# A new order of the first 520 steps in a fused attention and feed-forward kernel: two early holds and twelve more left out, two parts of w_in moved behind the third values

## The chip, the cores and the metric

The kernel runs on one core of a Trainium2 chip. The metric is the device time of one execution in microseconds (us), given as the median of several runs. The engines are TensorE (PE; PEld is its weight load), VectorE (DVE), ScalarE (ACT), GpSimd (POOL) and SyncE (SP). SP, POOL and, for three early transfers, ACT issue the DMAs; 16 DMA engines carry them.

## The reference

Inputs are q, k and v of 8 batches, 12 heads, 448 positions and 64 dimensions, w_in (768 x 2048) and w_out (2048 x 768), all float32; tau is 0.1.

```python
q_n = q / (norm(q, axis=-1) + 1e-6)
k_n = k / (norm(k, axis=-1) + 1e-6)
scores = q_n @ k_n.T / tau                # per batch and head, 448 x 448
attn = softmax(scores)
x = (attn @ v), heads side by side        # 3584 tokens x 768
h = x @ w_in
out = maximum(0.01 * h, h) @ w_out        # 3584 x 768
```

## The kernel before

Work goes by pairs of heads, 48 in all (s = 0 to 47, six in a batch), and by quads j of four heads. The first twelve pairs (two batches) use one layout, the later ones are loaded two pairs at a time as units. The feed-forward part goes by chunks c of tokens, two to a pair of batches: even chunks have 384 columns, odd ones 512.

Nothing is scheduled automatically. The string ORDER lists about 1,260 steps; the loop at the end of the kernel calls them one by one, and each engine runs its instructions in exactly that sequence. Semaphores only make an instruction wait for its data or for a buffer. So the order is the whole plan, and a waiting instruction holds up all that stands behind it on its engine. The steps, by name in ORDER:

- lq.s loads pair s of q and k on SP (from pair 12 on, the q or the k of two pairs), for s < 12 in four transfers (L238 to L241), later in two (L230). It uses a pool of four buffers, so a load waits until the normalise of an older pair has read its buffer. The pairs 0 to 5 are loaded ahead of ORDER (L211, L219, L220).
- lv.j and lr load the values and their last 64 rows, wi.i (L182) a quarter of w_in and wo.half (L188) half of w_out, or half of a half with a range; all on POOL. wi.0 and wi.1 hold the even and the odd row blocks (kt) of the columns m = 0 to 7, wi.2 and wi.3 those of m = 8 to 15. lg loads values for the later batches.
- sq.s.p squares on POOL (L306, later L300; p = 0 is q, 1 is k), sa on ACT; su sums on DVE (L319, L316). qf and uf do this for pair 0 in three pieces (L324, L330): main q (qf.0.0.3), main k (qf.1.0.3) and the last 64 rows of both (qf.0.3.4). ro.s takes the roots on ACT (L336, L337), no.s normalises on DVE into qn (L342 to L359).
- tp.s transposes on TensorE (L374), tc.s copies the result with DVE and ta with ACT (L390). k.s.i makes scores (L427), x.s.i the exps on ACT (L438). to.j and pr.j.e are the sums and products with the values on TensorE (L450), ln and in the inverse of the sums on ACT (L462, L466), sc.j.e scales into xT on DVE (L478).
- f.c.m and any kt behind it is the product with w_in (L588), r.c.m the leaky ReLU on ACT (L602), s.c.t.lo.hi the product with w_out (L624), o its copy out on DVE and the store on SP (L640, L648).
- q, y, g, gl, gi, gx, tt and td do the same as k, x, to, pr, ln, in, sc and the transposes for the units of the later batches.
- w.n are n matmuls on a constant tile (L695) whose result isn't used; tg lets TensorE's output banks be given out without a split in halves.
- hp.s is a hold: a copy of one element of the normalised pair s on POOL (L704), which makes what stands behind it on POOL wait for no.s. hs.s is the same for SP's queue, a transfer of one element (L701). hr reads an element of pair 0's remainder on POOL (L707).

```python
    def hold_loads(s):
        nc.sync.dma_start(out=behind, in_=qn[s][0:1, 6, 0, 0:1])

    def hold(s):
        gp.tensor_copy(out=seen, in_=qn[s][:, 6, 0, 0:1])
```

Of the kernel before, what the change touches and what calls it, by code (L numbers as in the profile page):

```python
# [764 lines left out]
```

## Time and profile before

| | |
|---|---|
| median of 3 runs | 414.89 us (414.45 to 415.11) |
| the profiled execution | 414.45 us |
| its span, first to last instruction | 412.7 us |
| TensorE busy | 403.0 us (98%) |
| granted TensorE clock | 1.00 throughout |
| ACT, DVE, POOL busy | 245.8, 262.2, 117.9 us |
| w_out's first half: issue, time to landing | 32.45, 22.97 us |
| first product with w_out (L624) | 55.47 us |

The span counts from the first instruction to the last; the execution's own time is 1.75 us longer. Busy time is the time in which an engine has at least one instruction in flight. In lists of instructions the columns are start, length, engine, line, operation and tiles, and behind "x" how many of them were merged; in brackets stands the idle time before and what ended it. In the list of waits the columns are the total, the number and the longest. In the chain that ended last each piece has a start and a length.

### The profile page before, as it was taken

The page shows a single profiled execution, that of the slowest core. Times are in us where ns is not written, and L with a number is a line of the kernel's source. Part 1 is how long each engine was busy: PE and PEld are TensorE (multiplying, and loading weights), DVE is VectorE, ACT ScalarE, POOL GpSimd, SP SyncE. Part 2 cuts the span into 40 slices and gives each one's busy share as a digit, 9 for nine tenths or more (in the row PEclk, how much of TensorE's full clock was granted, in tenths as well). Part 3 has the DMA queues.
Part 4 walks back from the last instruction along what each step waited for, and adds up shares of the span by engine and source line. Part 5 has one row for each costly group of instructions (what it writes and reads, how often), then busy time and mean ns, then how long its engine had stood idle before and what let it go on. Part 6 is the DMA issues. An engine that isn't in the chain of part 4 may idle for free.

```text
span 412.7 us, 11078 instructions
## 1 busy us (share of the span) xinstructions
PE 403.0 (98%) x4662; PEld 211.5 (51%) x4679; DVE 262.2 (64%) x424; ACT 245.8 (60%) x431; POOL 117.9 (29%) x125
## 2 busy tenths in 40 slices
PE   7899999999999999999999999999999999999997
PEld 2335555544555555544455555554455555554565
DVE  6987769757758556765484877699978591310021
ACT  4897886367937785667865679515854735104400
POOL 2978474164416032532240623330010000000000
PEclk9999999999999999999999999999999999999999
DMA  7999999767387852683555756382052210010032
GB/s 186 247 215 195 227 227 167 213 171 157 92 184 212 206 132 50 168 241 93 104 136 155 178 158 161 83 203 83 2 99 76 80 41 0 2 75 2 2 114 76
DMA packets 41976, 53.81 MB, mean 130 GB/s; under 512 B 12486, under 2 KB 32326, under 8 KB 41926
## 3 DMA queue, kind: packets, MB, share of 16 engines
q1 hardware_dynamic: 25734, 41.01, 35.7%
q0 software_dynamic: 15504, 11.80, 20.0%
q8 instruction: 36, 0.59, 0.6%
q10 hardware_dynamic: 688, 0.30, 0.2%
q14 instruction: 14, 0.11, 0.1%
HBM read 45.61 MB, written 11.01 MB: 137 GB/s over the span
## 4 chain that ended last, share of the span: by engine, by line
PE 83%; DMA 10%; DVE 3%; SPq 2%; issue 1%; POOL 1%; DVEq 0%
PE ps L624 33%; PE ps L588 32%; PE ps L538 8%; PE ps L492 7%; DMA w_out_sb<-in_moe_w_out_dram 6%; DMA qk_h<-in_q_dram 2%; PE ps L450 2%; DMA qk_h<-in_k_dram 1%; DMA xT<-in_q_dram 1%; DVE shared L508 1%; PE ps L524 1%; PE ps L427 1%; SPq L211 0%; SPq L219 0%; DVE qn L359 0%
## 5 line engine op out<-in xcount | busy, mean ns | idle before, releaser
L624 PE MATMUL ps<-w_out_sb,hT 128*128 128x384 bf16 (+1 forms) x912 | 151.7, 324 | 0.3 <-DMA w_out_sb<-in_moe_w_out_dram 0.3
L588 PE MATMUL ps<-xT,w_in_sb 128*128 128x384 bf16 (+1 forms) x753 | 149.4, 352 | 1.1 <-issue 0.5
L500 ACT ACTIVATE pe<-ps 128x896 bf16<-128x896 f32 x126 | 109.9, 917 | 54.4 <-PE ps L492 54.2
L624 PEld LDWEIGHTS <-hT 128*128 128x128 bf16 x912 | 86.4, 98 | 64.3 <-issue 10.1
L588 PEld LDWEIGHTS <-w_in_sb 128*128 128x128 bf16 x768 | 73.2, 98 | 73.4 <-issue 7.8
L602 ACT ACTIVATE hT<-ps 128x384 bf16<-128x384 f32 (+1 forms) x128 | 64.4, 549 | 62.1 <-PE ps L588 44.1
L300 POOL TENSOR_TENSOR sq<-qk_h 128x896 f32<-128x896 f32 x36 | 64.8, 1805 | 77.6 <-DMA qk_h<-in_q_dram 39.5
L640 DVE COPY osb<-ps 128x384 f32<-128x384 f32 (+1 forms) x57 | 30.7, 544 | 78.3 <-PE ps L624 74.7
L349 DVE TENSOR_TENSOR qn<-qk_h,r 128x896 bf16<-128x896 f32 x36 | 43.9, 1220 | 1.5
L316 DVE TENSOR_REDUCE ss<-sq 128x14 f32<-128x910 f32 x36 | 38.3, 1070 | 8.0 <-POOL sq L300 8.0
L438 ACT ACTIVATE pe<-ps 128x896 bf16<-128x896 f32 x42 | 36.3, 914 | 5.2 <-PE ps L427 5.1
L492 PE MATMUL ps<-qkT 64*32 64x448 bf16 x1008 | 36.0, 352 | 0.2 <-DVE osb L640 0.2
L508 DVE TENSOR_TENSOR shared<-shared,pe 128x896 f32<-128x896 f32 x30 | 35.5, 1215 | 0.3
L564 DVE TENSOR_TENSOR xT<-ps,rb 128x448 bf16<-128x448 f32 x32 | 18.3, 616 | 20.1 <-ACT rb L550 12.4
L400 DVE STREAM_TRANSPOSE tt<-qn 128x448 f32<-128x448 f32 x36 | 28.6, 812 | 0.5
L538 PE MATMUL ps<-pe,vq 64*32 64x448 bf16 x1008 | 27.0, 349 | 0.0
L704 POOL CAST seen<-qn 128x1 f32<-128x1 bf16 x21 | 6.6, 315 | 68.9 <-DVE qn L349 66.1
L492 PEld LDWEIGHTS <-qkT 64*32 64x32 bf16 x1008 | 12.6, 91 | 19.1 <-issue 14.7
L342 DVE TENSOR_REDUCE r<-norms 128x14 f32<-128x28 f32 x48 | 8.3, 174 | 21.7 <-ACT norms L337 21.1
L282 POOL DMA_DIRECT2D vq<-in_v_dram x20 | 12.6, 637 | 25.6 <-PE ps L492 25.6
L538 PEld LDWEIGHTS <-vq 64*32 64x32 bf16 x1008 | 14.6, 93 | 8.7 <-issue 0.6
L336 ACT ACTIVATE ss<-ss 128x14 f32<-128x14 f32 x48 | 10.3, 215 | 9.4 <-DVE ss L316 6.3
(55 smaller groups left out, 234.6 us busy)
## 6 DMA issues: line engine op xcount, KB each, us to landing
qk_h<-in_k_dram SPq DMA_DIRECT2D x36, 224.0 KB, 4.5
qk_h<-in_q_dram SPq DMA_DIRECT2D x36, 224.0 KB, 4.3
out_dram<-osb SPq DMA_DIRECT2D x20, 384.0 KB, 2.4
qkT<-tt SPq DMA_DIRECT2D x72, 56.0 KB, 2.0
qkT<-tt SPq DMA_DIRECT2D x36, 112.0 KB, 2.4
vq<-in_v_dram POOLq DMA_DIRECT2D x16, 224.0 KB, 5.0
w_in_sb<-in_moe_w_in_dram POOLq DMA_DIRECT2D x4, 768.0 KB, 9.6
out_dram<-osb SPq DMA_DIRECT2D x15, 192.0 KB, 3.4
```

Of the source, the lines that this page charges most:

```text
L300: gp.tensor_tensor(sq[:, :, :D], x, x, op=ALU.mult)
L316: nc.vector.tensor_reduce(o, sqs[s], axis=AX.X, op=ALU.add)
L349: nc.vector.tensor_tensor(qn[s].rearrange("p m d e -> p m e d"), raw[s].rearrange(f"p ({t[1:-1]} d) -> p m e d", e=n, d=D), r.rearrange(f" ...
L438: nc.scalar.activation(out=dst, in_=sc[:, :, :S], func=AF.Exp, scale=inv_tau)
L492: nc.tensor.matmul(out=sc[32 * strip : 32 * strip + 32, a, :S], lhsT=x[rows, c0 : c0 + 32], rhs=x[rows, 0:S], start=True, stop=True,)
L500: nc.scalar.activation(out=pq[u, i], in_=sc[:, :, :S], func=AF.Exp, scale=inv_tau)
L508: eng.tensor_tensor(whole[u], pq[u, 0] if i == 1 else whole[u], pq[u, i], op=ALU.add)
L538: nc.tensor.matmul(out=po[32 * strip : 32 * strip + 32, w, :S], lhsT=weights, rhs=pq[us[x if two else 0], i][rows, a, :], start=(i == 0), ...
L588: nc.tensor.matmul(out=pm[:, :n], lhsT=w_in_sb[:, kt, m * 128 : (m + 1) * 128], rhs=xT[c // 2][:, kt, c0 : c0 + n], start=(done + i == 0), ...
L602: nc.scalar.activation(out=hT[c][:, m, :n], in_=pm[:, :n], func=AF.Prelu, alpha=0.01)
L624: nc.tensor.matmul(out=po2[:, : hi - lo], lhsT=hT[c][:, m, ts * 128 : (ts + 1) * 128], rhs=w_out_sb[:, m, lo:hi], start=(m == 0), stop=(m ...
L640: nc.vector.tensor_copy(out=o[:, lo:hi], in_=bank(("s", c, ts, lo))[:, : hi - lo])
```

## The change

Only ORDER changes. Its first 534 steps become 520, from the start to the third batch's second unit (y.4.0 and all behind it are as before). Fourteen holds are left out: hp.1, 4, 8, 10, 11, 12, 13, 15, 17, 20, 22 and 23, hs.3 and hs.11. No other step is added or removed. The others are permuted, on every engine:

- The squares and sums of pair 0 begin with the last 64 rows (qf.0.3.4). ta.0.0.4 comes before ro.1.
- On POOL, lv.2, wi.3, sq.7.1, sq.6.0, wi.2 now follow sq.5.0 (before: hp.4, sq.6.0, lv.2, hr, hp.5, sq.6.1, sq.7.0, sq.7.1, wi.2, wi.3). lr.1.0.4 comes before sq.8.0 and wo.0 (before: behind wo.0 and lv.3). wo.1.0.8 comes before lv.3, and lv.4 behind wo.1.8.
- On SP, lq.9 follows lq.8 directly; lq.13 comes before lq.11; hs.9 stands behind lq.12 (before: ahead of lq.13 and lq.12).
- On DVE, no.4 comes before su.5.1; su.6 to su.8 all come before no.6; no.8 follows no.7 (before: no.9 was ahead of no.8).
- On ACT, ro.6 follows all exps of pair 5 (before: it was ahead of x.5.3), and ro.11 and ro.13 come before x.9.1 and r.0.15.
- On TensorE, the same steps stand ahead of the first product with w_out in both orders, but k.8.0 before and k.8.2 after; that first product is s.0.0.0.384 before and s.0.2.0.384 after.

The first lines of both orders (the diff's lines, cut behind the first products with w_out):

```diff
-qf.0.0.3 qf.1.0.3 uf.0.0.3 lq.6 qf.0.3.4 w.20 uf.1.0.3 uf.0.3.4 ro.0 sa.1.1 sq.2.1 sa.1.0 no.0 tp.0.4.7 su.1.0
-sq.2.0 su.1.1 tg tp.0.0.4 w.2 lr.0.0.2 ro.1 tc.0.4.7 su.2.1 lv.0 sq.3.1 no.1 su.2.0 w.2 ta.0.0.4 sq.3.0 lq.7
-k.0.1 lr.0.2.4 x.0.1 k.0.0 w.2 w.2 tp.1 k.0.2 x.0.0 w.2 tc.1 k.1.3 ro.2 no.2 su.3.0 su.3.1 x.0.2 k.1.2 x.1.3
-lv.1 k.1.1 x.1.2 x.1.1 ro.3 w.2 sq.4.1 k.1.0 tp.2 w.3 tc.2 k.2.1 k.2.2 k.2.0 x.1.0 su.4.1 to.0 x.2.2 pr.0.0
-no.3 hp.1 sq.4.0 su.4.0 x.2.1 x.2.0 ro.4 tp.3 w.2 wi.0 tc.3 ln.0 wi.1 sq.5.1 k.3.3 lq.8 su.5.1 k.3.2 k.3.1
-sq.5.0 w.2 no.4 su.5.0 hp.4 sq.6.0 x.3.3 lv.2 hr x.3.1 x.3.2 pr.0.1 tp.4 tc.4 k.3.0 ro.5 x.3.0 no.5 in.0 k.4.0
-k.4.1 hp.5 x.4.1 sc.0.0 sc.0.1 to.1 tp.5 k.4.2 ln.1 pr.1.1 pr.1.0 sq.6.1 sq.7.0 sq.7.1 tc.5 x.4.0 in.1 x.4.2
-sc.1.1 k.5.0 sc.1.0 k.5.2 hs.3 x.5.0 k.5.3 wi.2 x.5.2 f.0.1.0.2 f.0.0.0.2 k.5.1 x.5.1 wi.3 su.6.0 su.6.1
-su.7.1 f.0.1.1 f.0.1.3 f.0.0.1 ro.6 x.5.3 sq.8.0 wo.0 lv.3 f.0.2.0.1.2.3 f.0.3.0.1.2.3 to.2 pr.2.1 pr.2.0 lq.9
-ln.2 in.2 no.6 su.7.0 tp.6 sq.8.1 lq.10 sc.2.1 sc.2.0 f.0.6 sq.9.1 f.0.3.4.5 f.0.2.4.5 f.0.0.4.5 r.0.6
-f.0.1.4.5 ro.7 lr.1.0.4 r.0.2 sq.9.0 tc.6 su.8.0 su.8.1 no.7 k.6.2 k.6.0 r.0.3 f.0.4 f.0.5 x.6.2 sq.10.0 tp.7
-lq.11 sq.10.1 tc.7 r.0.1 su.9.0 su.9.1 f.0.0.3 f.0.7 r.0.4 x.6.0 r.0.5 r.0.0 ro.8 f.0.15 k.6.1 k.7.0 ro.9
-r.0.15 x.7.0 r.0.7 k.7.1 f.0.10 x.6.1 x.7.1 f.0.9 no.9 tp.9 r.0.9 r.0.10 tc.9 su.10.0 f.0.8 k.7.2 k.9.2 k.7.3
-su.10.1 x.9.2 lv.4 sq.11.1 f.0.12 f.0.11 r.0.8 ro.10 x.7.3 x.7.2 no.8 hs.9 no.10 hp.8 sq.11.0 f.0.13 f.0.14
-tp.8 r.0.13 r.0.11 lq.13 r.0.12 wo.1.0.8 r.0.14 k.9.1 tc.8 x.9.1 su.11.1 sq.13 k.9.0 to.3 su.11.0 ln.3 lq.12
-k.9.3 ro.11 k.8.0 x.9.3 x.9.0 x.8.0 tp.10 s.0.0.0.384 no.11 tc.10 k.8.1 k.10.1 k.8.2 sq.12 x.8.1 in.3 pr.3.1
-o.0.0.0.384 wo.1.8 hs.11 su.13 pr.3.0 ro.13 x.8.2 x.10.1 tp.11 s.0.1.0.384 hp.11 tc.11 k.11.0 sc.3.0 lv.5
-sc.3.1 su.12 k.11.1 k.11.2 x.11.0 x.11.1 s.0.2.0.384 lq.14 k.11.3 no.13 o.0.1.0.384 ro.12 x.11.2 k.10.2 k.10.0
-x.11.3 pr.4.1 hp.10 no.12 pr.4.0 x.10.0 to.4 x.10.2 hp.13 lq.15 sq.14 to.5 s.0.0.384.768 s.0.2.384.768 pr.5.1
-ln.5 su.14 tt.13 tt.12 ro.14 ln.4 in.4 in.5 pr.5.0 sq.15 su.15 o.0.2.0.384 no.14 td.0 lq.16 sc.4.0
-o.0.2.384.768 sc.4.1 sc.5.1 o.0.0.384.768 q.0.0 q.0.2 q.0.1 lq.18 ro.15 s.0.1.384.768 hp.12 sq.16 y.0.0 y.0.1
-y.0.2 tt.14 sc.5.0 no.15 f.1.12 f.1.15 f.1.11 f.1.1 lq.19 lq.17 r.1.12 tt.15 r.1.11 su.16 o.0.1.384.768 r.1.15
-sq.18 sq.17 sq.19 q.0.4 q.0.3 q.0.5 su.18 su.17 td.1 y.0.3 hp.15 lg.0 f.1.7 r.1.1 ro.16 no.16 y.0.4 r.1.7
...
+qf.0.3.4 uf.0.3.4 qf.1.0.3 uf.1.0.3 qf.0.0.3 uf.0.0.3 ro.0 no.0 sa.1.1 sa.1.0 sq.2.1 su.1.0 w.2 w.20 tp.0.4.7
+tc.0.4.7 su.1.1 su.2.1 sq.2.0 lr.0.0.2 tp.0.0.4 ta.0.0.4 w.2 w.2 lv.0 ro.1 w.2 sq.3.1 sq.3.0 lr.0.2.4 no.1
+sq.4.1 w.2 k.0.1 k.0.0 x.0.1 lq.6 x.0.0 w.3 su.2.0 tp.1 tc.1 lq.7 lv.1 ro.2 k.0.2 tg x.0.2 sq.4.0 k.1.1 k.1.2
+k.1.3 no.2 w.2 wi.0 su.3.1 x.1.2 x.1.3 x.1.1 w.2 su.3.0 tp.2 tc.2 w.2 su.4.1 ro.3 k.1.0 k.2.2 k.2.0 x.1.0 wi.1
+sq.5.1 sq.5.0 k.2.1 to.0 lv.2 x.2.2 x.2.0 no.3 su.4.0 wi.3 tp.3 x.2.1 pr.0.1 sq.7.1 sq.6.0 tc.3 k.3.2 wi.2
+ro.4 ln.0 x.3.2 k.3.1 k.3.0 pr.0.0 no.4 su.5.1 lq.8 su.5.0 hr x.3.0 lq.9 x.3.1 ro.5 tp.4 k.3.3 x.3.3 sq.6.1
+tc.4 k.4.0 in.0 x.4.0 no.5 sq.8.1 sq.7.0 lr.1.0.4 to.1 ln.1 sc.0.0 k.4.1 pr.1.0 k.4.2 in.1 sc.0.1 x.4.1 tp.5
+tc.5 pr.1.1 sc.1.0 k.5.3 f.0.1.0.2 sc.1.1 su.8.1 x.4.2 su.6.1 su.6.0 x.5.3 k.5.0 f.0.0.0.2 k.5.1 k.5.2 x.5.0
+x.5.1 f.0.0.1 f.0.1.3 f.0.1.1 f.0.3.0.1.2.3 f.0.2.0.1.2.3 su.7.0 su.7.1 x.5.2 sq.8.0 su.8.0 ro.6 to.2 pr.2.1
+pr.2.0 f.0.0.3 wo.0 no.6 tp.6 ro.8 ln.2 in.2 ro.7 sc.2.0 sc.2.1 f.0.7 r.0.7 f.0.0.4.5 f.0.3.4.5 f.0.2.4.5
+f.0.1.4.5 sq.9.0 sq.9.1 hp.5 tc.6 r.0.0 no.7 lq.10 r.0.1 k.6.1 k.6.0 no.8 f.0.6 sq.10.1 x.6.0 r.0.2 lq.13
+f.0.5 r.0.3 tp.7 su.9.1 wo.1.0.8 r.0.6 su.9.0 sq.10.0 r.0.5 x.6.1 lv.3 ro.9 f.0.4 tc.7 no.9 k.7.3 k.7.0 k.7.1
+r.0.4 x.7.3 tp.8 f.0.8 x.7.0 x.7.1 r.0.8 f.0.9 k.7.2 k.6.2 tp.9 tc.8 tc.9 su.10.1 f.0.11 su.10.0 lq.11 lq.12
+f.0.12 hs.9 f.0.10 x.7.2 x.6.2 sq.13 k.9.2 k.9.3 r.0.11 r.0.9 r.0.12 k.9.0 ro.10 no.10 wo.1.8 sq.11.1 to.3
+r.0.10 x.9.3 f.0.13 ln.3 sq.11.0 su.11.1 su.13 sq.12 x.9.2 f.0.14 lq.14 r.0.13 x.9.0 r.0.14 tp.10 k.8.2 k.9.1
+su.11.0 f.0.15 ro.11 no.11 ro.13 x.9.1 r.0.15 tc.10 s.0.2.0.384 x.8.2 tp.11 no.13 su.12 tc.11 o.0.2.0.384
+s.0.1.0.384 ro.12 k.11.2 k.11.1 lq.15 o.0.1.0.384 tt.13 no.12 x.11.1 x.11.2 k.8.1 s.0.0.0.384 k.8.0 sq.14 lv.4
+lv.5 x.8.1 in.3 k.10.1 x.8.0 k.10.0 pr.3.0 o.0.0.0.384 tt.12 sq.15 td.0 su.14 sc.3.0 lq.16 to.4 lq.18 pr.3.1
+x.10.1 k.11.0 x.10.0 ln.4 ro.14 k.11.3 k.10.2 sc.3.1 in.4 x.11.3 s.0.1.384.768 s.0.2.384.768 su.15 no.14 lq.17
+ro.15 x.11.0 sq.16 q.0.6 q.0.0 no.15 sq.18 x.10.2 pr.4.1 to.5 tt.14 y.0.0 y.0.6 o.0.2.384.768 sc.4.1 tt.15
+o.0.1.384.768 sq.17 pr.4.0 pr.5.1 ln.5 in.5 pr.5.0 sc.4.0 sc.5.1 sc.5.0 lg.1 td.1 lq.19 su.18 su.16 q.0.4
+q.0.3 q.0.1 y.0.1 s.0.0.384.768 ro.16 ro.18 y.0.4 su.17 f.1.8 o.0.0.384.768 r.1.8 q.0.2 q.0.5 no.16 no.18
...
```

More of the change, by code (lines that the diff above doesn't have):

```diff
@@ L97 @@
-o.7.3.384.576 s.7.3.576.768 o.7.3.576.768
+qf.0.3.4 uf.0.3.4 qf.1.0.3 uf.1.0.3 qf.0.0.3 uf.0.0.3 ro.0 no.0 sa.1.1 sa.1.0 sq.2.1 su.1.0 w.2 w.20 tp.0.4.7
[3 more added lines that the diff above has]
+sq.5.1 sq.5.0 k.2.1 to.0 lv.2 x.2.2 x.2.0 no.3 su.4.0 wi.3 tp.3 x.2.1 pr.0.1 sq.7.1 sq.6.0 tc.3 k.3.2 wi.2
@@ new lines @@
+o.4.2.384.768 a.13.1 a.12.4 a.13.2 o.4.1.384.768 f.5.11 f.5.2 f.5.7 f.5.9 f.5.0 sq.46 a.13.3 r.5.2 y.14.0
+f.5.4 r.5.9 r.5.0 f.5.3 f.5.6 a.13.4 a.13.5 ro.45 r.5.4 ro.44 su.47 r.5.7 r.5.11 r.5.3 no.45 su.46 a.12.5
+ro.46 td.15 a.13.6 a.12.6 r.5.6 q.14.4 q.14.1 q.14.3 y.14.4 f.5.14 f.5.5 no.46 no.44 q.14.5 y.14.1 y.14.3
+r.5.5 ro.47 r.5.14 q.15.0 g.7 f.5.12 f.5.13 gl.7 f.5.10 f.5.1 tt.45 no.47 y.15.0 r.5.12 r.5.13 y.14.5 gi.7
+q.15.1 q.14.6 g.7.0 y.15.1 a.14.1 y.14.6 tt.46 tt.47 a.15.1 tt.44 gx.7.0 f.5.15 f.5.8 q.15.3 q.15.4 r.5.10
@@ L98 @@
+s.6.2.384.768 r.7.0 r.7.9 f.7.7 f.7.10 f.7.3 f.7.2 r.7.3 f.7.5 r.7.2 r.7.10 r.7.5 f.7.1 r.7.15 r.7.1 f.7.6
+f.7.4 f.7.8 f.7.14 r.7.8 f.7.11 o.6.0.384.768 f.7.13 o.6.1.384.768 r.7.4 f.7.12 r.7.6 r.7.14 r.7.11 r.7.7
+r.7.12 r.7.13 s.7.0.0.384 o.7.0.0.384 s.7.0.384.768 o.7.0.384.768 o.6.2.384.768 s.7.1.0.384 o.7.1.0.384
+s.7.1.384.768 o.7.1.384.768 s.7.2.0.384 o.7.2.0.384 s.7.2.384.768 o.7.2.384.768 s.7.3.0.384 o.7.3.0.384
+s.7.3.384.576 o.7.3.384.576 s.7.3.576.768 o.7.3.576.768
 """
```

105 lines of the change are left out of this document (48 added, 57 removed).

## The prediction

> **What bounds the kernel now.** I read the page first, then TensorE's waits, the chain of waits, and the transfers by window.
>
> ```profile
> PE 403.0 (98%) x4662; PEld 211.5 (51%) x4679; DVE 262.2 (64%) x424; ACT 245.8 (60%) x431; POOL 117.9 (29%) x125
> DMA  7999999767387852683555756382052210010032
> ```
>
> TensorE is busy for 403.0 of 412.7 us: 9.7 us are idle. Its waits tell where.
>
> ```profile
> PE ps L695 <- DVE pe L678: 1.7, 1, 1.7
> PE ps L427 <- DVE qkT L390: 1.1, 2, 0.6
> PE ps L427 <- ACT qkT L390: 1.0, 1, 1.0
> ...
> PE ps L624 <- DMA w_out_sb<-in_moe_w_out_dram: 0.3, 1, 0.3
> ```
>
> The long ones lie before 26 us, in the warm-up (L695) and the first scores (L427). From 25.6 us on the timeline shows only two idle pieces above 0.2 us: 0.34 us at 55.47, for w_out, and 0.22 us at 274.78. In the window 36.06 to 55.13 TensorE is busy 19.07 of 19.07 us. So no order of the steps behind 26 us can gain much there; it can lose. The chain tells what the early part hangs on.
>
> ```profile
> 29.91 1.53 POOL w_in_sb L182 x2
> 31.56 0.89 issue
> 32.45 22.97 DMA w_out_sb<-in_moe_w_out_dram
> 55.47 2.77 PE ps L624 x16
> ```
>
> The first half of w_out (wo.0) is issued at 32.45, lands 22.97 us later, at 55.42, and the first L624 starts 0.05 us behind that. TensorE had arrived at 55.13. Two clocks meet here within 0.34 us: TensorE's work and the transfers. The transfers in the window 22 to 55.4:
>
> ```profile
> q0 software_dynamic: 4826, 4.98, 91.0%
> q1 hardware_dynamic: 2786, 2.18, 27.3%
> ```
>
> The columns are packets, MB and share of the 16 engines: they are full (118%, packets overlap). q0 holds what POOL issues, q1 what SP issues. Issue time plus time to landing gives q0's landings in the order of issue: wi.0 26.6, wi.1 31.3, lv.2 32.8, wi.2 37.2, wi.3 41.9, wo.0 55.4, lv.3 57.8, the four of lr.1 58.1 to 58.6. q0 is a line that doesn't run empty between 18.6 and 58.6: to issue a transfer earlier moves nothing unless what stands in front of it changes.
>
> **The change, part by part.**
>
> *First normalise.* The squares of pair 0 run main q, main k (L324, 3.96 and 4.43) and then the remainder, which lands at 5.32; the logarithm (L336) starts at 6.01. After, the remainder is first: 5.34, then two of 0.5 us to 6.6, then the last sum (0.56) to 7.2. no.0 comes 1.2 us later. Against this, ta.0.0.4 (ACT's copy of the transposed q) goes ahead of ro.1, which waits 1.23 us at 9.69: the copy starts at 10.06 though its transposes were done at 8.8. After, these end at 10.0 and the copy follows at once. The first exp starts at 11.1, as now (11.08). But no.1 goes from 10.30 to 11.25, and ACT's wait at ro.2 from 0.41 to between 0.7 and 1.4 us. ACT's next waits (0.15, 0.24, 0.52, for DVE and for scores) go for it, and no.4 in front of su.5.1 gives DVE 0.5 us back. ACT's 21 exps end at 33.5 now; I take 33.5 again, from 32.9 to 34.3.
>
> *Holds hp.1, hp.4, hs.3.* hp.1 takes 0.19 us and waited for nothing; wi.0 is issued 0.15 us sooner. hp.4 waited 2.27 us; but wi.3, wi.2 (0.8 us of issue each) and lr.1 (4 x 0.63) now come before sq.8.0, which ends at 32.6, as now (32.5). lq.9 is issued at 19.5 instead of 21.17.
>
> What the holds keep apart shows in the timelines of POOL and DVE (start, length):
>
> ```profile
> 17.61 1.04 POOL L306 TENSOR_TENSOR sq<-xT 128x512 f32<-128x512 f32 x1
> 18.52 1.82 DVE L359 TENSOR_TENSOR qn<-xT,r 128x512 bf16<-128x512 f32 x2
> 23.00 1.16 DVE L359 TENSOR_TENSOR qn<-xT,r 128x512 bf16<-128x512 f32 x2 [0.25 <-DVE r L343]
> ```
>
> A normalise that begins while POOL squares takes 1.82 us, one beside an idle POOL 1.16: a collision costs DVE 0.66 us (0.86 at 38.60). Without hp.4, no.5 and no.6 can each meet one. no.6 (now 32.74 to 34.39) waits for ro.6, now behind the last exp, and for su.8.0: it would start at 33.6 and, meeting sq.9.0, end at 36.0. TensorE needs tp.6 behind it at 35.8: 0.2 to 0.4 us lost.
>
> The Trainium skill (SBUF — State Buffer, section Who interferes with whom) says that a VectorE instruction with two SBUF inputs and a GpSimd instruction that reads SBUF exclude each other, whichever starts first. The rows above agree, and it speaks against leaving out holds; by it alone the sum would get 0.66 us for no.6 where I hide most of it.
>
> *w_in behind the third values.* wi.3 and wi.2 are issued at about 22.7 and 25.3 instead of 30.7 and 29.9, but in q0 they still stand behind wi.1 and lv.2, which land at 31.3 and 32.8. They land when they did. What counts is wi.1: the first product with odd kt starts at 31.38, right at its landing (31.33), and the set of steps ahead of it is the same after. wi.1 gains 0.15 us of issue and loses to lq.9, all of which now passes before it; the part that lands behind it now (to 32.5) is about a tenth to a fifth of lq.9's 2.2 us of engine time, 0.2 to 0.4 us. So +0.15 us. From there TensorE needs 23.75 us to the first L624 (31.38 to 55.13), and the same set again: arrival at 55.3, with tp.6's loss 55.6.
>
> *wo.0.* In front of it in q0 now stands lr.1, which today follows lv.3: four landings that end 0.83 us behind lv.3's. That is the first term: **+0.83**. The second is q1. 2.18 MB took 27.3% of 33.4 us, 9.1 us of engines, so 4.2 us per MB, or 3.5 with the overlap of 118%. lq.13, lq.11 and lq.12 are issued as their buffers come free, with hs.9 behind them instead of in front: at about 39.4, 41 and 45 instead of 46.2 (lq.13), 40.7 and 50.1 (lq.12). Today lq.12 lands at 57.3, so part of it passes wo.0's end; after, all of it passes before, and perhaps some of lq.14. Between 0 and one pair (0.46 MB): 0 to 1.6 us. I take **+0.6**, nearer to 0 since most of lq.12 is through by 55.4. wo.0 lands at 55.42 + 0.83 + 0.6 = 56.85 (55.6 to 57.9). TensorE, there at 55.6, waits 1.25 us, and the first L624 starts at 56.9 instead of 55.47: **+1.43 us**. The wait covers tp.6's loss and small stalls before it; without that cover they would count in full.
>
> The Trainium skill (DMA: Bandwidth & Descriptors, section Queues, rings and completion order) says that a DMA engine takes turns between the queues that hold work, packet by packet. By that, each pair load brought ahead of wo.0's end delays it by its whole engine time, and the second term would be 1.6 instead of 0.6; q0's rate in the rows (309 KB in a 2 us window with q1 busy, 387 to 412 without) falls by less than half.
>
> *Behind it.* s.0.2 to s.0.0 and the rest are 357.2 us (55.47 to 412.7), dense, with the same matmuls. The later holds (hp.8 to hp.23, 0.2 us each) free POOL, which is busy 29%. lv.3 moves behind wo.1.0.8 and, by q0's pace, lands at about 64 to 65.5; pr.3.0 needs it at 66.6. wo.1.8 lands at about 70 and is needed at 71. td.0 lands at 73.6, q.0.6 needs it at 75. All three are covered, by 1 to 2 us; I take 0, with up to 2 us of loss kept for the range, and below nothing no more than the 0.16 us of idle before 101.82.
>
> **Sum.** 412.7 + 1.43 = 414.1 of span; the profiled execution took 414.45, so 415.9. It was the lowest of the three runs; their median, 414.89, gives 416.3 us.
>
> **Rivals.**
> *The transfers are not later* (not slower than before). q0 moves 165 to 206 GB/s in the windows without q1 and both together 203 to 245 (24 to 32 and 40 to 56 us). lq.9 now fills 22 to 24 us, where q1 was empty. If loads brought forward ride in such gaps, the second term is 0 or negative (0.5 us at most), and lr.1, four small transfers, could pass beside lv.2 or the w_in parts for less than 0.83. Then wo.0 lands near 55.4 and TensorE is there at 55.3 to 55.6: +0.0 to +0.8 us, 414.9 to 415.7. It decides if wo.0 lands by 55.9. For it: the 118%. Against: nothing leaves q0's line in front of wo.0.
> *Faster by the earlier products.* sc.1.0 comes before sc.1.1, so f.0.1.0.2 can start near 29.2 instead of 30.2. That pays 1.0 us only if wi.1 lands by 30.4 and wo.0 by 54.4; 413.9. Nothing in q0 goes that way.
> *A second wait behind w_out.* ro.11 and ro.13 stand in front of r.0.15 on ACT. lq.11, behind lq.13, gets its last two transfers out when earlier ones land (SP's issue at 5.33 follows the landing at 5.32), near 45, and with 8.9 us to landing comes at 54.2; sq.11.0, su.11.0, ro.11, ro.13, x.9.1 and r.0.15 take 3.9 us: 58.1. s.0.2's last matmul needs it at 56.9 + 15 x 0.163 = 59.3. Beyond 1.2 us of delay it costs one for one; with lv.3 or wo.1.8 late as well, 1 to 3 us more: 417.3 to 419.5.
>
> **How the numbers follow.** Forecast (w_out 0.9 to 2.3 us later, 415.8 to 417.2): 0.48. Second wait: 0.20. Transfers not later: 0.23. Faster: 0.09. The range leaves out the faster case and the upper end of the second wait: 414.7 to 418.6. About 0.2% (0.83 us) is what a measurement here tells from no change: faster by more 0.09, within 0.24, slower 0.67.
>
> **What would show it.** Right: the chain still has wo.0 in front of the first L624, with a wait of TensorE of about 1 us; wo.0's landing near 56.9, behind lr.1's; wi.2 and wi.3 landing between 36 and 43 in spite of their early issue; the first exp at 11.1 and the last at 33 to 34. Wrong: a first L624 before 55.3 (then the transfers were not the limit), or idle TensorE above 0.5 us behind 57 (then the later order is).

## The result, and the profile after

The changed kernel takes **420.51 us** (median of 6 runs, 419.83 to 423.84) against 415.0 for the kernel before (6 runs, 414.45 to 415.95): a ratio of 1.0152, 95% interval [1.0116, 1.0189]. Forecast were 416.3 and a range up to 418.6: the sign was right, the size far off, and the range did not hold it. The profiled execution, the second longest of the six and the only one with a timeline, took 423.14 us with a span of 421.4; pieces read from it add up to more than the median shows. The page's busy times and granted clock:

```profile
PE 408.3 (97%) x4679; PEld 212.8 (51%) x4679; DVE 271.2 (64%) x424; ACT 246.6 (59%) x431; POOL 111.9 (27%) x113
PEclk9779999999999999999999999999999999999999
```

TensorE does the same work (it had 403.0 us) and is busy 5.3 us longer; the clock row shows two slices of 7. DVE, at the same 424 instructions, is busy 9.0 us longer (262.2 before). TensorE's list of waits has a new first line, the transposes behind the normalise; none for w_out is left:

```profile
PE ps L373 <- DVE qn L358: 5.1, 3, 2.4
PE ps L694 <- DVE pe L677: 1.7, 1, 1.7
PE ps L426 <- DVE qkT L389: 1.3, 3, 0.5
PE ps L426 <- DVE xT L477: 1.1, 1, 1.1
```

(L358 is the old L359; most lines moved up by one.) The timeline of DVE shows no.1, no.2 and no.3, two pieces each:

```profile
11.70 3.77 DVE L358 TENSOR_TENSOR qn<-xT,r 128x512 bf16<-128x512 f32 x2
...
17.09 2.79 DVE L358 TENSOR_TENSOR qn<-xT,r 128x512 bf16<-128x512 f32 x2
...
22.35 3.75 DVE L358 TENSOR_TENSOR qn<-xT,r 128x512 bf16<-128x512 f32 x2
```

Beside an idle POOL both take 1.16, so these lose 2.6, 1.6 and 2.6 us. Before, they took 1.79, 1.75 and 1.82 (the third row is shown in the prediction):

```profile
10.79 1.79 DVE L359 TENSOR_TENSOR qn<-xT,r 128x512 bf16<-128x512 f32 x2
...
14.20 1.75 DVE L359 TENSOR_TENSOR qn<-xT,r 128x512 bf16<-128x512 f32 x2
```

POOL at the time of the first, in the changed kernel:

```profile
12.40 0.79 POOL L255 DMA_DIRECT2D shared<-in_v_dram  x1
13.20 1.84 POOL L305 TENSOR_TENSOR sq<-xT 128x384 f32<-128x384 f32 x2
14.98 1.30 POOL L263 DMA_DIRECT2D shared<-in_v_dram  x2
```

The second piece of no.1 starts at 12.53, while POOL issues lv.0, and ends at 15.47: it waited through the rest of the issue and both squares, and its own 0.55 us fit in only from 14.92, just before POOL issues lr.0.2.4 (14.98). POOL's order here is that of before; there the piece began at 11.39, during the issue of lr.0.0.2, and ended at 12.58, before the squares (12.82). The squares come 0.4 us later than before, the piece 1.1 us later, and so it meets them. At no.3 it is the hold: the squares from 23.83 to 25.67 that its second piece (from 23.33) waits for are sq.7.1 and sq.6.0, and hp.4 kept the like behind no.4. The Trainium skill (SBUF — State Buffer, section Summary: rules for kernel authors) says that of a VectorE instruction with two SBUF inputs and a GpSimd one that reads SBUF the second to issue blocks until the first finishes. The measurement differs: the piece began at 12.53, ahead of both squares (13.20 and 14.00), and waited for both.

What the late no.1 does to TensorE, in its timeline:

```profile
9.80 1.89 PE L694 MATMUL ps<-pe 128*128 128x512 bf16 x8
...
15.53 0.34 PE L373 MATMUL ps<-id,qn 128*128 128x128 bf16 x3 [2.37 <-DVE qn L358]
...
18.04 1.89 PE L694 MATMUL ps<-pe 128*128 128x512 bf16 x4
```

Before, the idle time in front of the same transposes was 0.21 us:

```profile
12.63 0.34 PE L374 MATMUL ps<-id,qn 128*128 128x128 bf16 x3 [0.21 <-DVE qn L359]
```

Behind the gap of 2.37 us four warm-up matmuls take as long as eight did ahead of it. The busy time by windows (columns: stretch, length, busy time and instructions, granted clock, DMA share, GB/s):

```profile
9.40:16.00 6.60, 4.23 (x31) 1.00 1.15 250
16.00:22.80 6.80, 6.36 (x31) 0.50 1.19 249
22.80:26.20 3.40, 1.54 (x23) 1.00 1.07 195
26.20:29.60 3.40, 3.40 (x29) 0.50 1.14 210
29.60:61.60 32.00, 31.49 (x341) 1.00 1.25 218
```

Behind the gaps of 2.37 us (to 15.53) and 1.86 us (to 26.15) the clock is at half for 6.8 and 3.4 us. The Trainium skill (TensorE: Matmul & The Clock Gate, section Why this matters for your kernels) warns of idle gaps over about 3 us. Here gaps of 1.9 and 2.4 us were enough in one execution, so the measurement differs.

The first product with w_out:

```profile
61.62 2.76 PE L623 MATMUL ps<-w_out_sb,hT 128*128 128x384 bf16 x16
```

It comes 6.15 us later than before and waits for nothing. w_out's first half had landed at 53.43, earlier than the 55.42 of before. From s.1.3.384.768 on both kernels do the same steps; that one starts at 133.76 before and at 142.01 after. Of these 8.25 us, 4.41 are TensorE's longer busy time up to there (132.59 instead of 128.18, by the windows view; the half clock) and 3.84 its idle time (9.42 instead of 5.58). By place, 6.15 us are there at the first product with w_out, and 2.10 come behind it. The longest idle piece there:

```profile
75.43 0.76 PE L426 MATMUL ps<-qkT 64*64 64x448 bf16 x12 [1.09 <-DVE xT L477]
```

The scaling that these scores wait for (sc.3.0) stands on DVE behind no.12, and no.12 took 3.10 us from 69.52, with a square on POOL from 69.87 to 71.57, where no.13 had taken 1.16 us at 64.99 beside an idle POOL. Of the six runs, the two with a mean granted clock below 0.993 took 423.1 and 423.8, the others (0.995 to 1.00) 419.8 to 420.9.

### The profile page after: what moved, and what is told of

Read it like the earlier page. It is cut to its first block, busy times and chain, and to the rows that moved or that the text cites. A ratio compares the mean times of both kernels' runs of the same rounds, so it can differ in the third digit from the quotient of the medians.

```text
span 421.4 us, 11070 instructions
## 1 busy us (share of the span) xinstructions
PE 408.3 (97%) x4679; PEld 212.8 (51%) x4679; DVE 271.2 (64%) x424; ACT 246.6 (59%) x431; POOL 111.9 (27%) x113
## 4 chain that ended last, share of the span: by engine, by line
PE 85%; DVE 7%; DMA 3%; SPq 2%; ACT 1%; issue 1%; POOL 0%; POOLq 0%; DVEq 0%
PE ps L587 34%; PE ps L623 31%; PE ps L537 8%; PE ps L491 6%; DVE qn L358 4%; PE ps L449 2%; PE ps L426 2%; SPq L408 1%; DMA qk_h<-in_q_dram 1%; DMA qkT<-tt 1%; DVE ss L315 1%; DMA xT<-in_q_dram 1%; DVE ss L318 1%; PE ps L373 1%; DVE qkT L389 1%
## 5 line engine op out<-in xcount | busy, mean ns | idle before, releaser
L587 PE MATMUL ps<-xT,w_in_sb 128*128 128x384 bf16 (+1 forms) x768 | 151.6, 353 | 0.5 <-DVE xT L563 0.5
L299 POOL TENSOR_TENSOR sq<-qk_h 128x896 f32<-128x896 f32 x36 | 63.3, 1763 | 110.4 <-DMA qk_h<-in_k_dram 54.9
L348 DVE TENSOR_TENSOR qn<-qk_h,r 128x896 bf16<-128x896 f32 x36 | 46.9, 1303 | 1.3
L507 DVE TENSOR_TENSOR shared<-shared,pe 128x896 f32<-128x896 f32 x30 | 34.5, 1183 | 0.3
L341 DVE TENSOR_REDUCE r<-norms 128x14 f32<-128x28 f32 x48 | 8.4, 175 | 22.9 <-ACT norms L336 22.1
L426 PE MATMUL ps<-qkT 64*64 64x448 bf16 (+1 forms) x132 | 13.7, 394 | 2.4 <-DVE qkT L389 1.3
```

The lines of the kernel that those rows point to most:

```text
L299: gp.tensor_tensor(sq[:, :, :D], x, x, op=ALU.mult)
L348: nc.vector.tensor_tensor(qn[s].rearrange("p m d e -> p m e d"), raw[s].rearrange(f"p ({t[1:-1]} d) -> p m e d", e=n, d=D), r.rearrange(f" ...
L507: eng.tensor_tensor(whole[u], pq[u, 0] if i == 1 else whole[u], pq[u, i], op=ALU.add)
L587: nc.tensor.matmul(out=pm[:, :n], lhsT=w_in_sb[:, kt, m * 128 : (m + 1) * 128], rhs=xT[c // 2][:, kt, c0 : c0 + n], start=(done + i == 0), ...
```

## The experiments

Times of landmarks are from the profiled execution of each kernel; "common" is the start of the first of the common steps, s.1.3.384.768. Ratios are to the kernel before, run beside each on the same chip (414.3 to 415.4). What each kernel is stands in the sections below.

| kernel | median us | ratio | first exp | no.3 ends | first w_out product | common |
|---|---|---|---|---|---|---|
| before | 415.0 | | 11.08 | 20.34 | 55.47 | 133.76 |
| after | 420.51 | 1.0152 [1.0116, 1.0189] | 12.03 | 26.10 | 61.62 | 142.01 |
| h1 old head | 420.15 | 1.0129 [1.0087, 1.0170] | 10.86 | 20.29 | 57.65 | 138.83 |
| h2 new head | 419.41 | 1.0122 [1.0059, 1.0185] | 13.02 | 22.72 | 58.90 | 137.95 |
| e1 | 419.25 | 1.0123 [1.0077, 1.0168] | 10.68 | 21.53 | 57.18 | 139.87 |
| e2 | 417.04 | 1.0050 [1.0018, 1.0081] | 11.33 | 20.21 | 54.74 | 133.16 |
| e3 | 421.10 | 1.0155 [1.0105, 1.0204] | 11.81 | 23.50 | 62.63 | 141.93 |
| c1 | 415.75 | 1.0017 [0.9991, 1.0042] | 10.60 | 20.18 | 56.41 | 135.35 |
| e4 | 422.51 | 1.0145 [1.0067, 1.0224] | 11.69 | 25.18 | 60.65 | 140.98 |
| e5 | 419.58 | 1.0116 [1.0091, 1.0142] | 14.30 | 23.27 | 62.63 | 142.05 |
| p0 bank kept | 423.24 | 1.0188 [1.0137, 1.0239] | 11.92 | 25.94 | 66.34 | 145.76 |
| p1 + r in it | 418.14 | 1.0077 [1.0057, 1.0097] | 11.79 | 19.23 | 56.51 | 137.49 |
| l1 | 419.33 | 1.0117 [1.0093, 1.0141] | 11.03 | 20.20 | 59.29 | 138.31 |
| ml | 417.04 | 1.0057 [1.0039, 1.0076] | 10.91 | 20.79 | 56.49 | 135.94 |
| ml2 | 416.46 | 1.0053 [1.0027, 1.0080] | 10.76 | 20.04 | 56.34 | 135.60 |
| q0 | 421.15 | 1.0166 [1.0127, 1.0205] | 12.63 | 22.44 | 58.83 | 137.76 |
| q1 | 418.09 | 1.0078 [1.0052, 1.0104] | 12.01 | 19.45 | 58.05 | 137.67 |
| s1 | 414.84 | 0.9993 [0.9973, 1.0013] | 11.04 | 20.22 | 55.47 | 133.76 |
| q2 | 417.77 | 1.0070 [1.0047, 1.0094] | 12.27 | 19.70 | 58.11 | 137.10 |
| q3 | 418.09 | 1.0087 [1.0073, 1.0101] | 10.54 | 19.42 | 57.17 | 136.09 |

### Parts of the change, put back or done alone

e1 is the changed kernel with the old order of the first squares:

```diff
-qf.0.3.4 uf.0.3.4 qf.1.0.3 uf.1.0.3 qf.0.0.3 uf.0.0.3 ro.0
+qf.0.0.3 qf.1.0.3 uf.0.0.3 qf.0.3.4 uf.1.0.3 uf.0.3.4 ro.0
```

> The changed kernel with one thing put back: pair 0's squares and sums run main q, main k, remainder, as before; all holds stay out. Theory P (phase): the remainder first delays no.0 by 1.2 us and no.1 by as much, into a run of POOL squares, and VectorE's normalise then waits until that run ends; with the old first squares no.1 starts near 10.4 us, its two multiplications take at most 1.9 us together instead of 3.8, no.2 and no.3 likewise, and the time falls from 420.5 to 415 to 417 us. Theory H (holds): it is the missing holds that let POOL run into the normalises; then no.1 may be shorter but no.2 or no.3 stay at 2.8 to 3.8 us and the time stays above 418.5. Theory W (transfers, the one of the prediction): the first product with w_out is then limited by w_out again, at 56 to 57 us.

e2 is the kernel before with the new order of these (lq.6 w.20 behind them). e3 is the changed kernel with hp.1 in front of sq.4.0, hp.4 behind no.4 with lv.2 wi.3 sq.7.1 sq.6.0 wi.2 behind it, and hs.3 in front of lq.9.

> The kernel before with one part of the change: remainder first in pair 0's squares and sums; all holds stay in. Theory P: no.1 moves from 10.3 to about 11.5 us and meets the squares of pair 3 on POOL; one or more of no.1 to no.3 take over 2.5 us for their two multiplications, and the time rises by 2 to 5 us, to 417 to 420. Theory H: the holds keep POOL off, no more than the 1.2 us of delay is seen, 415 to 416.2.

> The changed kernel with hp.1, hp.4 and hs.3 put back, and lv.2, wi.3, sq.7.1, sq.6.0 and wi.2 behind hp.4. Theory P: no.1 and no.2 collide as in the changed kernel (3.8 and 2.8 us), no.3 perhaps not, since its squares of pairs 6 and 7 now wait for no.4; the time falls by 0 to 2.5 us, to 418 to 420.5. Theory H: back to 415 to 416.5.

e1 brought no.3 to 21.53. Its median is 1.3 us lower, which the intervals don't part, and no.2 still took 3.10 us, as theory H had it. Its profile shows a gap of 2.04 us at 65.11: the copy of pair 11's transposes stands on DVE behind no.13, which took 2.54 us at 61.01 beside a square, and behind su.12; half clock follows. e2 had a profiled run of 413.71, but its ten runs go from 413.7 to 421.1, and their median of 417.04 lies at the lower end of theory P. In the profiled run no normalise lost more than 0.7 us; no trace shows what the longer runs met. e3 gained nothing: with the holds no.2 and no.3 lost 0 and 0.75 us, but no.1 still 2.6 and no.5 1.5, and TensorE's gaps of 2.4 us moved to 15.3 and 60.9. So neither part alone carries the loss. By these traces it counts where the squares happen to lie when a normalise starts, and each edit moves that.

c1 tried to make a collision in the kernel before: lr.0.0.2 behind lq.7 k.0.1, so that only the issue of lv.0 stands between the squares of pair 2 and those of pair 3. The pieces of no.1 moved as well (10.42 to 11.58) and met no square: nothing follows for the cause. e4 splits the rows of squares in the changed kernel by a DMA issue:

```diff
-sq.3.1 sq.3.0 lr.0.2.4
+sq.3.1 lr.0.2.4 sq.3.0
-sq.7.1 sq.6.0 tc.3 k.3.2 wi.2
+sq.7.1 wi.2 sq.6.0 tc.3 k.3.2
```

> The kernel before with one POOL step moved: lr.0.0.2 (two issues) goes behind the squares of pair 3, so that the second multiplication of no.1 (11.4 us), which waits 0.63 us for one more issue to begin today, finds two squares in a row behind the issue it waits for. If VectorE gets its turn only when POOL's row of squares ends, that piece takes 2 to 2.6 us instead of 1.18, no.1 ends at 13.5 to 14.2 instead of 12.6, and the time rises by 0.5 to 2.5 us. If VectorE only waits for the instruction that POOL is in, it takes at most 1.4 us and the time stays within 0.5 us.

> The changed kernel with the two rows of squares broken by an issue: sq.3.1, lr.0.2.4, sq.3.0, and sq.7.1, wi.2, sq.6.0. If VectorE's turn comes with the first issue behind a square, the second multiplications of no.1 and no.3 take about 1.0 us less each (2.9 and 2.8 us now), and the time falls by 1 to 3 us, to 417.5 to 419.5. If the wait ends with POOL's next idle time instead, they stay or get longer.

The second piece of no.1 took 2.17 instead of 2.94 us in e4: it waited for one square, not two. But no.2 and no.3 still lost 2.3 and 2.1 us at other squares, and the median did not fall; 417.5 to 419.5 had been expected.

### The collisions taken away

A tensor_tensor with r in PSUM has one operand in SBUF. e5 put the r of pairs 0 to 5 into the spare columns of a bank that the warm-up matmuls also use, and cut these matmuls to 448 columns:

```diff
+    r_ps = ps[:, 7, 448:462]
-        nc.vector.tensor_reduce(r, norms[s % 3], axis=AX.X, op=ALU.add)
+        rr = r_ps if s < NPAIR else r
+        nc.vector.tensor_reduce(rr, norms[s % 3], axis=AX.X, op=ALU.add)
```

> The changed kernel with its order untouched, but for pairs 0 to 5 the factors r of the normalise lie in PSUM (14 unused columns of a bank) instead of SBUF, and the warm-up products are 448 instead of 512 columns wide. If VectorE waits because its second SBUF operand and POOL's squares exclude each other (theories P and H both rest on it), the two multiplications of no.1 to no.5 take 1.16 to 1.4 us each although POOL's squares lie beside them, and the time falls by 3.5 to 6 us, to 414.5 to 417. If the waits come from something else (a dependence between the steps, the slower clock), the normalises of 2.8 to 3.8 us and 419 to 421 us stay.

All pieces took 0.69 and 0.55: the second of no.1 ran from 12.81 to 13.36, inside a square (12.70 to 13.54). But the warm-up matmuls now waited for no.1 (1.83 us at 13.42), the first exp came at 14.30, and the median stayed at 419.58 where 414.5 to 417 had been expected. So the cause was confounded; p0 and p1 part it. In both the bank is kept out of the deal until no.5; in p1 it holds r of pairs 0 to 4.

```diff
-    age, taken = [0] * 8, {}
+    age, taken = [0] * 8, {"r": (7, 1)}
+        if s == 5:
+            give("r")
```

> The changed kernel with one bank of PSUM (the eighth) kept out of the deal until no.5; nothing else. It is the control of the next one. Every theory: the same waits of the normalises of pairs 1 to 3 as in after (in all 6 to 7 us beyond 0.69 and 0.55 in the first 26 us); the median equal to after's 420.5 or up to 1.5 us above it, if three banks for the single tiles are too few.

> The kernel of p0_after_one_bank_kept with the reciprocal norms r of pairs 0 to 4 in that kept bank of PSUM instead of SBUF, so that the normalises of these pairs have one operand in SBUF and one in PSUM, and no matmul writes the bank. Theory P (half of the loss is VectorE waiting for GpSimd's squares at no.1 to no.3): the pieces take 0.69 and 0.55 beside the squares, no.3 ends 3 to 5 us earlier than in the control (near 21 to 23), the first w_in product starts near 31 to 33 instead of 36, and the median falls by 2 to 4 us below the control; the rest of the loss, from the middle and the later loads, stays. Rival (the collisions only fill time in which these steps would wait anyway, for values, transposes or exps): the pieces shorten, the first w_in product moves by less than 1 us, and the median stays within 1 us of the control.

DVE in p0:

```profile
11.57 3.76 DVE L361 TENSOR_TENSOR qn<-xT,r 128x512 bf16<-128x512 f32 x2
...
16.95 2.79 DVE L361 TENSOR_TENSOR qn<-xT,r 128x512 bf16<-128x512 f32 x2
...
22.21 3.74 DVE L361 TENSOR_TENSOR qn<-xT,r 128x512 bf16<-128x512 f32 x2
```

and in p1, where the second piece of no.1 (12.06 to 12.60) again begins while POOL issues lv.0 (11.73 to 12.53), with the same two squares behind it (12.53 to 14.37):

```profile
11.45 1.15 DVE L361 TENSOR_TENSOR qn<-xT,ps 128x512 bf16<-128x512 f32 x2
...
14.41 1.15 DVE L361 TENSOR_TENSOR qn<-xT,ps 128x512 bf16<-128x512 f32 x2
...
18.07 1.15 DVE L361 TENSOR_TENSOR qn<-xT,ps 128x512 bf16<-128x512 f32 x2
```

The waits are gone, no.3 ends 6.7 us sooner, and the median falls by 5.1 us, from 423.24 to 418.14; by the ratios, whose intervals don't touch, it is 1.1% or 4.6 us. The runs also close up: 417.3 to 418.5 instead of 420.1 to 427.3, since the granted clock stays at 0.999 or more (0.984 in p0's longest). So the waits cost time, as theory P has it, and its rival (within 1 us of the control) fell. Both went further than expected: theory P gave 2 to 4 us, and the control at most 1.5 us above the changed kernel, where it came out 2.7 us above, which the intervals don't part. The one run of p0 at full clock took 420.06, and the changed kernel's two at 0.999 or more 419.83 and 419.95. By these three runs, none of them with a timeline, about 2 us are the waits themselves and the rest the half clock behind them.

Against the changed kernel itself p1 gains 2.4 of the 5.5 us. It is still 0.8% (3.2 us) above the kernel before, and its profile shows two large pieces of that: TensorE waits 1.01 us at 32.79 for wi.1, and 2.15 us at 64.87 for the copy of pair 11, which stands behind no.13. That one took 2.65 us from 60.65, beside a square (60.61 to 62.29): only pairs 0 to 4 have r in the bank.

### Head and rest

h1 does the steps of before up to f.0.1.0.2, and then the changed kernel's (lq.9, sq.8.1 and lr.1.0.4, which the old head lacks, stand directly in front of f.0.1.0.2); h2 the other way round.

> The steps up to the first product with w_in (f.0.1.0.2) stand as in the kernel before, with hp.1, hp.4 and hs.3; all other steps as in the changed order. Theory N (normalises): the loss is made in the first 30 us, where VectorE's normalises wait for POOL's squares; then the first product with w_out starts at 55.5 to 57 us and the time is 415 to 416.5. Theory L (late order): lq.11 behind lq.13 makes no.11 and its scores late, so TensorE still loses 1 to 3 us between 60 and 80 us; then 416.5 to 419. The prediction's term, lr.1 and more loads ahead of w_out: the first product with w_out at 56 to 57 instead of 55.5.

> The counterpart: the changed order up to f.0.1.0.2 (no hp.1, hp.4, hs.3 in it), the rest as in the kernel before. Theory N: f.0.1.0.2 starts at 33 to 36 us instead of 30.2 and the time is 417.5 to 421, most of the changed kernel's loss. Theory L alone: 415 to 416.

Each half alone costs 1.2 to 1.3%, the whole 1.5%: both count, and they overlap. (At the common steps it is 5.1 and 4.2 us, and 8.25 together, but the last in an execution with half clock.) h2 lies where theory N had it; h1's median is above what either theory gave, 419 at most. What the later half does shows in h1, first on DVE:

```profile
31.84 2.69 DVE L317 TENSOR_REDUCE ss<-sq 128x6 f32<-128x390 f32 x5 [2.10 <-POOL sq L304]
35.39 0.69 DVE L317 TENSOR_REDUCE ss<-sq 128x8 f32<-128x520 f32 x1 [0.85 <-POOL sq L304]
...
36.48 2.00 DVE L357 TENSOR_TENSOR qn<-qk_h,r 128x512 bf16<-128x512 f32 x2
```

then on POOL and TensorE:

```profile
31.75 2.54 POOL L262 DMA_DIRECT2D shared<-in_v_dram  x4
34.30 1.05 POOL L304 TENSOR_TENSOR sq<-qk_h 128x512 f32<-128x512 f32 x1
```

```profile
37.23 0.40 PE L372 MATMUL ps<-id,qn 128*128 128x128 bf16 x4 [1.71 <-DVE qn L357]
38.54 0.34 PE L372 MATMUL ps<-id,qn 128*128 128x128 bf16 x3 [0.92 <-DVE qn L357]
...
61.23 0.34 PE L622 MATMUL ps<-w_out_sb,hT 128*128 128x384 bf16 x1 [0.98 <-ACT hT L600]
...
65.58 0.84 PE L425 MATMUL ps<-qkT 64*64 64x448 bf16 x12 [0.66 <-DVE qkT L388]
```

The sums of pair 8 stand in front of no.6 on DVE and wait for their squares: su.8.1 for 2.10 us, for sq.8.1 (to 31.81), which stands behind the issues of wi.2 and wi.3 on POOL, and su.8.0 for 0.85 us, for sq.8.0, which stands behind four issues (lr.1, 2.54 us). no.6 ends at 38.49 instead of 34.39, and TensorE is idle for 2.63 us. In the changed kernel itself these sums ran without a wait (36.62 to 39.90), since all came later there. The last two rows are r.0.15 behind ro.11 and ro.13, and pair 11 loaded behind pair 13: the rival of a second wait. l1 mends these two, ml the middle as well, ml2 two sums that still stood in the way:

```diff
 l1 (on h1):
-lq.13 ... lq.11 ... sq.13 ... sq.11.1 ... ro.11 no.11 ro.13 x.9.1 r.0.15
+lq.11 ... lq.13 ... sq.11.1 ... sq.11.0 sq.13 ... r.0.15 ro.11 no.11 ro.13 x.9.1
 ml (on l1):
-lr.1.0.4 ... su.8.1 ... sq.8.0 su.8.0 ro.6 ... no.6 tp.6 ro.8
+ro.6 sq.8.0 ... no.6 su.8.1 su.8.0 tp.6 ... ro.8 lr.1.0.4
 ml2 (on ml):
-su.13 ... su.11.0 / su.8.1 su.8.0 ... sc.2.1
+su.11.0 ... r.0.15 ro.11 su.13 / sc.2.1 su.8.1 su.8.0
```

> The steps of before up to f.0.1.0.2 and those of after from there, as in h1_before_head_after_rest, but in the later part lq.11 stands where lq.13 stood and the other way round, sq.11 is in front of sq.13, and r.0.15 in front of ro.11. Theory L (behind the head, loss comes from pair 11 loaded behind pair 13, and from the relu r.0.15 queued behind the roots of 11 and 13): the idle pieces of TensorE at 61.2 us (0.98, waiting for hT) and at 65.6 (0.66, waiting for qkT of pair 11) go, no.11 ends near 57 to 58 instead of 61.9, and the median falls by about 1.6 us from 420.2 to 418.5. Rival (the middle, no.6 behind the squares of pair 8, is all that counts, the later waits are its echo): these idle pieces shrink by less than half, median within 0.5 us of 420.2.

> The same, and in the middle the sums of pair 8 (su.8.1, su.8.0), the roots ro.8 and the four remainder loads lr.1.0.4 moved behind no.6, so that no.6 doesn't wait for the squares of pair 8. Theory M (in the later part no.6 is late since DVE waits 2.1 and 0.85 us for squares of pair 8 that stand on POOL behind lr.1): no.6 ends near 35 instead of 38.5, the two idle pieces of TensorE at 37.2 and 38.5 us (1.71 and 0.92) go, and with L mended too the order costs little: the steps common to both kernels begin near 134 to 135 and the median is 415 to 416.5. Rival (the later order is bad for a reason spread over it, not for these waits): the named idle pieces go and others come in their place, median over 417.5.

> As ml_old_head_both_mended, but su.13 behind su.11.0 and ro.11 (it stood in front of su.11.0 and made VectorE wait 1.91 us for the squares of pair 13), and su.8.1, su.8.0 and ro.8 behind sc.2.1 (they stood in front of sc.2.0). Theory (the rest of the loss of the later part is again VectorE's place in line): the idle pieces of TensorE at 37.7, 38.2 and 63.3 us (0.40, 0.21, 0.66) go, no.11 ends near 57, the common steps begin at 134 to 134.7 instead of 135.9, and the median is 415.0 to 415.8. Rival (spread over the order): other pieces take their place, median 416.5 or more.

l1 took away the 0.98 us but not the wait for pair 11 (0.63). Its median is 0.8 us lower, where 1.6 us had been expected, and the intervals don't part the two. In ml the 2.63 us at no.6 shrank to 0.61, and the median fell by 2.3 us more: theory M holds, though 417.04 is above its upper end of 416.5. Its DVE shows what kept pair 11 late:

```profile
55.75 1.10 DVE L314 TENSOR_REDUCE ss<-sq 128x14 f32<-128x910 f32 x1 [1.91 <-POOL sq L298]
```

That is su.13, in front of su.11.0. With it moved (ml2) 0.63 us of TensorE's 0.66 stayed: su.11.0 now ends at 54.4, but ro.11 stands behind r.0.15, which waits on ACT to 56.54, the place where l1 had put it. One queue's wait had become another's. ml2's median of 416.46 lies between its theory (to 415.8) and its rival (from 416.5), and the ratios (1.0053 and 1.0057) don't part it from ml.

### The changed kernel with all of it mended

q0 has the mends of the later places in the changed kernel, q1 also r in the kept bank, s1 is the kernel before without hs.3, q2 is q1 with hs.3 in front of lq.9, and q3 is q2 with the warm-up behind the first scores:

```diff
 q3 (on q2):
-ta.0.0.4 w.2 w.2 lv.0 ro.1 w.2 sq.3.1 ... w.2 k.0.1 k.0.0 x.0.1
+ta.0.0.4 lv.0 ro.1 sq.3.1 ... k.0.1 k.0.0 w.2 w.2 w.2 w.2 x.0.1
```

> The changed kernel with its own head, and with the same mends in the middle (squares and sums of pair 8, lr.1.0.4) and later (lq.11 before lq.13, sq.13 and su.13 behind those of pair 11, r.0.15 before the roots of 11). Theory of two causes: the head's loss stays (no.3 ends near 26, TensorE's gaps near 15 and 26 us and the half clock behind them), the later one goes: the median falls from 420.5 to 417 to 419. Rival (with the late head the later places hardly count, since all comes later there): the median stays at 420 or more.

> The same with r of pairs 0 to 4 in the kept bank of PSUM, so that the collisions go as well. Theory of two causes: nothing of size is left, the first w_out product starts near 55.5, the common steps begin at 134 to 135.5, and the median is 415 to 416.5. Rival (something else in the new head costs: the remainder first, w_in's early parts, seven banks): the later idle pieces go, but the first w_in product still starts over 31 us and the median stays at 417 or above.

> The kernel before with one step left out: hs.3, the wait on SP's queue for no.3 in front of the loads of pair 9 (lq.9). Theory W (lq.9 passing beside w_in's first two parts delays them): lq.9 is issued from 18.9 instead of 21.2 us, wi.0 lands near 28 instead of 26.6 and wi.1 near 32.5 to 33 instead of 31.3; TensorE, which began the first even product at 30.2 and the first odd one at 31.4, waits 1 to 1.5 us there, and the median rises by 0.5 to 1.5 us over before. As predicted on record (0.15 us): wi.1 lands within 0.3 us of 31.3 and the median is within 0.5 us of before.

> The kernel of q1_changed_both_mended with hs.3 back in front of lq.9. Theory W: wi.1 lands at 31.3 to 32 instead of 32.9, TensorE's wait for it falls from 0.93 us to under 0.3, and the median falls from 418.1 to 416.8 to 417.5. Rival: wi.1 stays at 32.5 or later (then it is late for what stands in front of it in its own queue), median within 0.5 us of 418.1.

> The kernel of q2_changed_mended_load_hold with the four warm-up steps w.2 that stand in front of the first scores k.0.1 put behind k.0.0; as many matmuls as before. Theory (the eight warm-up matmuls of 0.22 us hold the first scores up): the scores follow the copy of q and k at once, near 10.9, the first exp starts at 11.3 instead of 12.27, the 21st exp ends 0.7 to 1 us sooner than 34.80, and the median falls by 0.5 to 1 us from 417.8. Rival (the squares' order sets it): the first exp stays over 11.8, or it comes earlier and the 21st exp ends within 0.3 us of 34.8, with a median within 0.4 us of 417.8.

q0's median, 421.15, is no better than the changed kernel's: with the late head the later places do not count, as its rival had it. Its profiled run, the shortest of six (418.89), met squares too, but with waits of 0.1 to 0.8 us each, 4.1 us in the first 30 (6.8 in the changed kernel's), and a full clock; its other runs took up to 424.3. q1 takes 3.1 us off q0, but nothing off p1 (418.09 against 418.14): its theory of two causes fell short by 1.6 us. The 2.15 us of p1 shrank to 0.63, but the first product with w_out came 1.5 us later than in p1.

s1: without hs.3, wi.1 landed 0.5 us later (31.83), TensorE waited 0.83 us for it, and w_out's first product still started at 55.47; the 0.34 us that it had waited there were gone. The time is that of before. Theory W fell, and so did q2's (417.77, though TensorE no longer waited for wi.1, landed 31.77).

q3: the first exp starts at 10.54 instead of 12.27, but ACT then waits for the next pair:

```profile
10.54 1.71 ACT L438 ACTIVATE pe<-ps 128x896 bf16<-128x896 f32 x2
12.97 0.21 ACT L333 ACTIVATE ss<-ss 128x14 f32<-128x14 f32 x1 [0.72 <-DVE ss L316]
...
13.86 2.70 ACT L438 ACTIVATE pe<-ps 128x896 bf16<-128x896 f32 x3 [0.43 <-PE ps L427]
```

The 21st exp ends 1.0 us earlier (33.81), the common steps begin 1.0 us earlier, and the median does not follow (418.09). **Open** is what the last 3 us of q1 to q3 are. Of the 2.3 us that q3's profile is late at the common steps 1.5 are idle time of TensorE in many pieces, of which 0.3 to 0.9 us each wait for exps or roots between 18 and 28 us; whether that comes from the kept bank or from the order was not parted. Nor are all collisions gone: from pair 5 on r lies in SBUF, and no.5 lost 1.0, 2.5 and 1.1 us in q1, q2 and q3. No run has r of all pairs in PSUM. No version came out below the kernel before.

## Why the prediction was wrong, point by point

- *First normalise.* no.1 was to begin at 11.25 and did (11.21). **Here the prediction failed:** it took ACT's 21 exps to end at 33.5, "as now", and they ended at 39.62. It had read the price of a collision, 0.66 us, from rows where a DMA issue followed the square, and it looked for collisions only at no.5 and no.6. In the changed kernel three of them cost 2.6, 1.6 and 2.6 us at no.1 to no.3, on a chain where no.1 feeds the transposes, the scores and the exps. p1 against p0 shows that these waits and what follows from them cost 4.6 us there by the ratios; against the changed kernel itself p1 gains 2.4 of the 5.5 us.
- *The first exp at 11.1* came at 12.03. The copy by ACT ended at 10.59, as worked out; but eight warm-up matmuls, put in front of the first scores by the new order, held TensorE from 9.80 to 11.62. They were queued on the engine and left out of the working. q3 shows that they set that time, and not that the time of the kernel hangs on it.
- *Holds.* no.6, put at 36.0 and 0.2 to 0.4 us of loss, ended at 41.65 (38.49 with the old head in h1, with 2.63 us of idle TensorE). su.8.0 had been named as a condition; that it waits for a square behind lr.1's 2.5 us of issue on POOL, and su.8.1 for one behind wi.2 and wi.3, had not been followed through. These waits show in h1; in the changed kernel no.6 was late since the exps, and ro.6 behind them, were. hs.3 alone costs nothing that the runs can tell (s1).
- *w_in.* Right in that wi.3 and wi.2 landed when the line let them, at 37.52 and 41.25, 14 to 16 us after their issue. wi.1 was 1.6 us late, not 0.15; that was covered, since TensorE came later still. With the head mended it was not (1.01 us in p1).
- *wo.0.* The two terms that made up the forecast, 0.83 and 0.6 us of transfers, measured nothing in the changed kernel: TensorE came at 61.62 and not at 55.6, and w_out lay there from 53.43. lr.1 did land in front of it, the last at 42.05. The later pair loads waited for the late no.6, which would have left the engines to w_out; that is argued, not tested. In p1, whose head is not late, w_out landed at 55.94, 0.52 us later than before instead of 1.43, and TensorE, there at 56.51, did not wait for it.
- *Behind it.* Taken as 0, and this term failed as well: 2.10 us came between the first product with w_out and the common steps (2.69 in p1, 2.89 in h1). In the changed kernel they are mostly idle pieces of TensorE, the longest 1.09 us, the prediction's own sign of being wrong; it came behind a collision at no.12, where the working had looked for none.
- *Rivals.* The mechanism of a second wait is there (h1, l1), in the place named, but mending it brought 0.8 us of the median, which the intervals of h1 and l1 don't part, and nothing under the late head (q0). *Transfers not later* had w_out's landing right (by 55.9) and the time wrong, since it too had TensorE there by 55.6. *Faster* did not come: the first product with w_in started at 36.03. The clock had no place in the working, though TensorE's busy time is 4.41 us longer by it in the profiled run. It isn't the whole: the two runs at 0.999 or more still lose 4.9 us.

## What to carry to other kernels

When an order moves, lay each two-operand VectorE instruction beside what GpSimd does at that moment and behind it: the price here was the whole row of squares up to GpSimd's next DMA issue, not one of them. Follow the chain from the first tile to the first full engine before reasoning on transfers that are needed later, and count the filler on each engine's queue. A gap on TensorE can cost more by the clock behind it than by itself (2.37 us here, and then 6.8 us at half clock); and a mend that moves a waiting instruction only counts if nothing needed stands behind its new place.
